# Adding epsilon to the softmax row sums on ScalarE instead of VectorE, and idle matrix products of 64 rows instead of 128

## The chip, the cores and the metric

The kernel runs on one core of one Trainium2 chip. The metric is the device time of one execution in microseconds (us), the median of several runs. A core has five engines that work side by side, each through its own list of instructions in order: TensorE (PE in the profile; PEld are its weight loads), VectorE (DVE), ScalarE (ACT), GpSimd (POOL) and SyncE (SP, which here only issues transfers). They wait for each other through semaphores. TensorE writes to PSUM, which has eight banks of 128 partitions by 512 fp32 words; everything else lies in SBUF.

## The reference

Three stages follow each other, in fp32:

```python
# attention: q, k, v of shape (2, 8, 1152, 64); q is averaged over pairs of tokens first
q_pool = q.reshape(B, H, S // 2, 2, D).mean(axis=3)
scores = matmul(q_pool, k.T) / sqrt(D)
attn = exp(scores - scores.max(-1))
attn = attn / (attn.sum(-1) + 1e-09)
x = matmul(attn, v)                      # then (1152, 512): tokens by heads
# gated MLP, d_ff 1536
x = (silu(x @ w_gate) * (x @ w_val)) @ w_out
# second MLP, d_ff 2048, with a slope alpha below zero
h = x @ w_in
out = (maximum(h, 0) + alpha * minimum(h, 0)) @ w_out2
```

The change is about the `+ 1e-09`, and about products that compute nothing.

## The kernel before, in words

**The order of the work.** The program doesn't issue instructions as it goes through its loops. Each step is handed to a planner (`Plan`, by `add`): engine, guessed duration, priority, what it reads and writes, and a function that emits the instructions. `Plan.run` then plays through time with these guesses and emits every step in the order in which it started in that play. TensorE's steps go strictly by priority. The other engines take the best step that is ready, or hold still for a better one if it will be ready within a short time (0.217 us for ACT, 0.095 us for DVE). A step given to `EITHER` (L730) goes to ACT or DVE, whichever is free. On the chip the order of each engine is then fixed; only the waits decide when a step runs.

**Attention** goes over eight pairs of heads (pair 0 to 7). The planner knows a shared resource between DVE and POOL: a step with `port=True`, and every POOL step, holds it alone. For one pair:

- `prep` loads q, k, v and splits q and k into a high and a low part for products of higher precision. For pair 0 this is done by ACT and DVE, for the others by POOL: L608 writes the high part, L616 the low part (for k these are tiles of 128x1152).
- `unit` computes scores of 128 queries by 1152 keys: matrix products L686 (and L678) into PSUM, then L692 on DVE (scaling, row minimum, copy into SBUF), then L696 on ACT (exp, with the row sum written by ACT into one column of `allsums`).
- `transposed` transposes the exps 64 keys at a time by products with the identity (L716), and ACT (L731) or DVE (L726) copies each filled bank back to SBUF as `et` and `eu`.
- `values` multiplies them with v (L751); ACT copies the result out (L755).
- `inverses` runs once per pair when the last exp of the pair has left its sum: L762 adds epsilon to the 128x9 sums on DVE, L763 takes the reciprocal on DVE into `allinv`, L764 transposes it on TensorE, L765 copies it to SBUF on ACT, and SP sends it through DRAM so that it comes back spread over partitions (L769, L772). `finish` multiplies (L781 on POOL; for the last pair L779 on DVE).

**The idle products.** Until the first `values` step is placed, TensorE gets a product of zeros into bank 7 whenever no step of its own is ready in the play (`plan.idle`, guessed at 0.12 us). It is `idle(256)`: 256 columns, 128 rows, bf16. Ahead of all steps stand 20 products `idle(512)` (`K["warm"]`). Nothing reads what they write.

**The two MLPs** follow from 210.7 us on, with weights that ACT and DVE rebuild from 64-bit words (L527 to L535) beside the products L842, L902 and L931.

Of the kernel before, what the change touches and what calls it, by code (L numbers as in the profile page):

```python
# [9 lines left out]
F32 = mybir.dt.float32  # L10
F32R = mybir.dt.float32r
I32 = mybir.dt.int32
AF = mybir.ActivationFunctionType
ALU = mybir.AluOpType
# [3 lines left out]
P = 128  # L18
PE, ACT, DVE, POOL, SP = "PE", "ACT", "DVE", "POOL", "SP"
# [68 lines left out]
class Plan:  # L88
# [34 lines left out]
    def buf(self, cls):  # L123
        b = Buf()
        c = self.classes[cls]
        b.cls, b.n, b.users, b.slot, b.until = cls, len(c["bufs"]), 0, None, 0.0
        c["bufs"].append(b)
        c["open"] += 1
        return b


    def add(self, eng, dur, emit, prio, reads=(), writes=(), bufs=(), extra=0.0, port=False, late=0.0, hold=0.0, cold=2.0, kind=None):
        t = Task()
        t.kind = kind
        t.eng, t.dur, t.extra, t.emit, t.prio = eng, dur, extra, emit, prio
        t.n, t.ways = len(self.tasks), None
        t.port, t.late = port or eng == POOL, late
        t.after, t.done, t.start, t.hold, t.cold = [], None, None, hold, cold
        deps = set()
        for k in reads:  # L140
            deps.update(self.wr.get(k, ()))
        for k in writes:
            deps.update(self.wr.get(k, ()))
            deps.update(self.rd.get(k, ()))
        for k in writes:
            self.wr[k] = [t]
            self.rd[k] = []
        for k in reads:
            self.rd.setdefault(k, []).append(t)
        deps.discard(t)  # L150
        t.left = len(deps)
        for d in deps:
            d.after.append(t)
        t.ready = 0.0
        t.bufs = list(dict.fromkeys(bufs))
        for b in t.bufs:
            b.users += 1
        self.tasks.append(t)
        return t
# [158 lines left out]
def tp(n):  # L318
    return n * 0.109 / 128.0
# [15 lines left out]
def act(n, sbuf=False, acc=False):  # L335
    return n / 1200.0 + (0.093 if sbuf else 0.051) + (0.186 if acc else 0.0)
# [15 lines left out]
def attention_moe_moe2(  # L352
# [13 lines left out]
    nc = tc.nc  # L366
    NP, _, _, SQ = qt.shape
    S = kt.shape[2]
    D = vt.shape[4]
# [5 lines left out]
    EPS = 1e-9  # L375
# [12 lines left out]
    const = ctx.enter_context(tc.tile_pool(name="const", bufs=1))  # L388
# [5 lines left out]
    signs = const.tile([P, 2, NF2], F32, name="signs")  # L394
    tiny = const.tile([P, 1], F32, name="tiny")
    nc.gpsimd.memset(tiny, 1e-10)
    xh = const.tile([P, KC, NT], F32R, name="xh")
    xl = const.tile([P, KC, NT], F32R, name="xl")
    bank = psum.tile([P, 8, 512], F32, name="bank")
# [4 lines left out]
    zeros = const.tile([P, 512], mybir.dt.bfloat16, name="zeros")  # L404
    nc.vector.memset(zeros, 0.0)

    def idle(n):
        nc.tensor.matmul(bank[:, 7, :n], zeros[:, :P], zeros[:, :n], start=True, stop=True)  # L408

    for i in range(K["warm"]):  # L410
        idle(512)

    plan = Plan()
    plan.first = K["begin_at"]
    plan.cold = K["cold"]
    plan.idle = lambda: idle(256)
    add, buf = plan.add, plan.buf


# [337 lines left out]
    def inverses(x, pos, rd):  # L757

        rows_ = []

        t, r9 = buf("s"), buf("r9")
        add(DVE, 0.097, lambda: nc.vector.tensor_scalar(x.sums.ap, x.sums.ap, EPS, None, ALU.add), pos, rd, [x.sums], [x.sums])  # L762
        add(DVE, 0.097, lambda: nc.vector.reciprocal(x.inv.ap[:, :NU], x.sums.ap), pos, [x.sums], [x.inv], [x.sums, x.inv])  # L763
        add(PE, tp(P), lambda: nc.tensor.transpose(t.ap[:, :P], x.inv.ap, ident), pos, [x.inv], [t], [t, x.inv])  # L764
        add(ACT, act(P), lambda: nc.scalar.activation(r9.ap, t.ap[:NU, :P], AF.Copy), pos, [t], [r9], [t, r9])  # L765
        for j in range(2):
            for dst, src in ((lambda j=j: x.row.ap[j:j + 1, :D], lambda j=j: r9.ap[0:1, j * D:j * D + D]),
                             (lambda j=j: x.row.ap[j, D:].rearrange("(u p) -> u p", p=P), lambda j=j: r9.ap[1 + 4 * j:5 + 4 * j])):
                add(SP, 0.5, lambda dst=dst, src=src: nc.sync.dma_start(dst(), src()), pos, [r9], [(x.row, j, dst)], [x.row, r9], extra=0.02)  # L769
                rows_.append((x.row, j, dst))  # L770
        for j, h in enumerate((slice(0, D), slice(D, P))):
            add(SP, 0.5, lambda j=j, h=h: nc.sync.dma_start(x.rr.ap[h], x.row.ap[j].partition_broadcast(D)), pos, rows_, [(x.rr, j), (x.rr, "q")], [x.rr, x.row], extra=0.41)  # L772
# [16 lines left out]
    for p in range(NP):  # L789
        x = prep(p)  # L790
        x.sums, x.inv, x.row = buf("sums"), buf("inv"), buf("row")
        ets = [[[buf(cls) for cls in ET] for _ in range(2)] for _ in range(2)]
        for g in ets:
            for h in g:
                for b in h:
                    b.parts = []
        xs = buf("xs")
        at = 0
        for g in range(2):
            for n in (OF if p else OF0)[g]:  # L800
                pos = 4.0 * p + 4.0 * (at + 0.5 + 0.5 * (n > 0)) / 9
                at += 1 + (n > 0)
                kinds, es = unit(x, p, n, pos)
                transposed(x, p, n, kinds, es, ets[g], pos)
            if g == 1:
                inverses(x, pos + rank("inv", p, 0), [(x.sums, n) for n in range(NU)])
            values(x, g, ets[g], xs, 4.0 * p + 2.0 * g + 1.0)
        finish(x, p, xs, 4.0 * p + 4.0 + rank("fin", p, 0))
# [201 lines left out]
```

## Time and profile before

| what | value |
|---|---|
| median of 3 runs | 642.7 us (642.59 to 643.03) |
| the profiled execution | 642.54 us |
| its span in the trace | 640.7 us (1.84 us lie outside it) |
| busy share: PE, DVE, ACT, POOL | 99%, 75%, 52%, 16% |
| mean granted TensorE clock | 0.997 of full speed |

The span is the time from the first to the last recorded instruction. Busy time of TensorE is modelled from pipelined products, so 99% says that it has nearly always something in flight, not that it runs at its peak. The profile names a line, an engine, the tiles written and read (`out<-in`), a count, and in brackets the idle time of that engine ahead of it with what ended it.

### The profile page before, as it was taken

Reading aid. Unit: us, or ns where it says so; the run is one execution under the profiler, and the core shown is the slowest. Engines: PE = TensorE matmul, PEld = TensorE weight load, DVE = VectorE, ACT = ScalarE, POOL = GpSimd, SP = SyncE. Lnnn points to the kernel's source line nnn. Section 1 sums busy time; section 2 is a strip of 40 time slices with the busy share of each in tenths; the row PEclk is TensorE's granted clock in tenths of the full one; section 3 lists DMA queues with packets and bytes.
Section 4 is the critical chain, followed back from the end, with each engine's and each line's share of the span. In section 5 each row is a group of like instructions: output and inputs, shape, how many; then the busy total and the mean of one; then the engine's idle time right before and its main releaser. Section 6 shows DMA issues by size and latency. Waiting matters only on the chain.

```text
span 640.7 us, 12340 instructions
## 1 busy us (share of the span) xinstructions
PE 634.6 (99%) x4901; PEld 557.8 (87%) x4901; DVE 478.6 (75%) x1012; ACT 334.9 (52%) x604; POOL 104.4 (16%) x114
## 2 busy tenths in 40 slices
PE   9989999999999999999999999999999999999998
PEld 5777777777776999999999999999988898899886
DVE  6898988988889999988548866688996299463332
ACT  4858887887889535445334222313864454342210
POOL 4543554456204000000000000051000000000000
PEclk9989999999999999999999999999999999999999
DMA  6222322221133434352311420113124011000012
GB/s 223 75 85 85 95 85 85 95 94 39 58 112 107 150 131 132 135 194 72 128 66 68 178 84 19 47 66 132 66 99 165 0 67 67 0 1 2 0 50 98
DMA packets 16874, 55.37 MB, mean 86 GB/s; under 512 B 2160, under 2 KB 3120, under 8 KB 16816
## 3 DMA queue, kind: packets, MB, share of 16 engines
q1 hardware_dynamic: 16672, 54.35, 24.8%
q8 instruction: 38, 0.62, 0.4%
q14 instruction: 20, 0.16, 0.1%
q10 hardware_dynamic: 144, 0.23, 0.1%
HBM read 52.17 MB, written 2.40 MB: 85 GB/s over the span
## 4 chain that ended last, share of the span: by engine, by line
PE 97%; ACT 1%; DVE 1%; issue 1%; DVEq 0%; ACTq 0%
PE bank L842 39%; PE bank L931 16%; PE bank L902 12%; PE bank L751 11%; PE bank L686 9%; PE bank L716 7%; PE bank L678 2%; PE bank L408 2%; ACT plain L696 1%; DVE allsums L762 0%; ACT spare L696 0%; PE bank L764 0%; ACT et L731 0%; DVE plain L692 0%; DVE plain L939 0%
## 5 line engine op out<-in xcount | busy, mean ns | idle before, releaser
L842 PE MATMUL bank<-xh,weights 128*128 128x384 f32 x960 | 253.3, 337 | 0.0
L842 PEld LDWEIGHTS bank<-xh,weights 128*128 128x128 f32 x960 | 174.4, 188 | 2.2 <-issue 0.4
L842 PE MATMUL bank<-xl,weights 128*128 128x384 f32 x480 | 161.4, 336 | 0.0
L842 PEld LDWEIGHTS bank<-xl,weights 128*128 128x128 f32 x480 | 90.2, 188 | 1.2
L696 ACT ACTIVATE plain<-plain,stats 128x1152 f32<-128x1152 f32 x51 | 63.8, 1254 | 15.8 <-DVE plain L692 15.8
L931 PE MATMUL bank<-wr,fed 128*128 128x512 f32 (+1 forms) x279 | 70.4, 387 | 0.0
L686 PE MATMUL bank<-fed 64*128 64x448 f32 (+1 forms) x576 | 65.0, 356 | 0.1
L882 ACT ACTIVATE plain<-bank,signs 128x384 f32<-128x384 f32 x48 | 27.9, 581 | 69.5 <-PE bank L842 69.3
L931 PEld LDWEIGHTS bank<-wr,fed 128*128 128x128 f32 x279 | 51.1, 188 | 10.4
L692 DVE TENSOR_SCALAR_CACHE_REDUCE plain<-bank,stats 128x448 f32<-128x448 f32 (+1 forms) x102 | 55.9, 580 | 2.1 <-PE bank L686 0.9
L883 DVE SCALAR_TENSOR_TENSOR plain<-bank,signs,plain 128x384 f32<-128x384 f32 x48 | 29.5, 614 | 36.2 <-ACT plain L882 36.2
L686 PEld LDWEIGHTS bank<-fed 64*128 64x128 f32 x576 | 48.4, 189 | 6.1 <-issue 1.6
L902 PE MATMUL bank<-fed,wr 128*128 128x384 f32 x264 | 52.2, 338 | 0.0
L716 PEld LDWEIGHTS bank<-ident,plain 64*128 64x128 f32 x918 | 37.9, 139 | 11.4 <-issue 5.5
L911 POOL TENSOR_SCALAR xh<-plain 128x384 fp32r<-128x384 f32 x12 | 13.3, 1110 | 206.8 <-DVE plain L909 206.8
L902 PEld LDWEIGHTS bank<-fed,wr 128*128 128x128 f32 x264 | 46.8, 188 | 0.0
L716 PE MATMUL bank<-ident,plain 64*128 64x64 f32 x918 | 43.5, 228 | 1.7 <-DVE eu L726 1.6
L931 PE MATMUL bank<-wr,h 128*128 128x512 f32 (+1 forms) x165 | 44.3, 389 | 0.0
L527 ACT ACTIVATE magnitudes<-plain 128x1024 f32<-128x1024 f32 x34 | 38.8, 1143 | 9.7 <-DMA plain<-in_w_in 4.5
L751 PE MATMUL bank<-et,plain 128*64 128x320 f32 (+1 forms) x320 | 42.8, 412 | 0.0
L530 DVE SCALAR_TENSOR_TENSOR magnitudes<-plain,magnitudes 128x1024 int32<-128x1024 int32 x34 | 41.4, 1217 | 0.2
L531 DVE SCALAR_TENSOR_TENSOR magnitudes<-plain,magnitudes 128x1024 int32<-128x1024 int32 x34 | 41.4, 1217 | 0.2
(83 smaller groups left out, 936.8 us busy)
## 6 DMA issues: line engine op xcount, KB each, us to landing
plain<-in_w_out SPq DMA_DIRECT2D x28, 512.0 KB
plain<-in_w_in SPq DMA_DIRECT2D x16, 512.0 KB
plain<-in_w_gate SPq DMA_DIRECT2D x12, 512.0 KB
plain<-in_w_val SPq DMA_DIRECT2D x12, 512.0 KB
plain<-in_vt SPq DMA_DIRECT2D x8, 576.0 KB
plain<-in_qt SPq DMA_DIRECT2D x7, 576.0 KB
plain<-in_kt SPq DMA_DIRECT2D x7, 576.0 KB
plain<-rowd SPq DMA_DIRECT2D x16, 144.0 KB
```

The lines of the kernel that those rows point to most:

```text
L527: add(ACT, act(2 * DM, True), lambda: nc.scalar.activation(mag.ap, word(1, F32), AF.Abs), prio, reads=got, writes=[mag], bufs=[raw, mag])
L530: add(DVE, dve(2 * DM), lambda: nc.vector.scalar_tensor_tensor(bits(), word(0, I32), 29, bits(), ALU.logical_shift_right, ALU.bitwise_or), ...
L531: add(DVE, dve(2 * DM), lambda: nc.vector.scalar_tensor_tensor(bits(), word(1, I32), -0x40000000, bits(), ALU.bitwise_and, ALU.bitwise_or) ...
L686: nc.tensor.matmul(ss[h].ap[:, :w], x.qhl.ap[rows, a * SQ + c0:a * SQ + c0 + P], x.khl.ap[rows, b * S + js.start:b * S + js.stop], start=k ...
L692: add(DVE, dve(w) + (0.067 if i else 0.01), lambda s=s, js=js, w=w, i=i, m=m, e=e: nc.vector.tensor_scalar(e.ap[:, js], s.ap[:, :w], QSCAL ...
L696: add(ACT, act(S, True, True), lambda e=e, st=st, u=u: nc.scalar.activation(e.ap, e.ap, AF.Exp, bias=st.ap[:, NCUT - 1:NCUT], scale=-1.0, ...
L716: nc.tensor.transpose(ts[h].ap[:, c * D:c * D + D], e.ap[rows, ks:ks + P], ident[rows, rows])
L751: nc.tensor.matmul(acc.ap[rows, :n], x.vn.ap[:, h * SQ + kc * D:h * SQ + kc * D + D], ets[h][blk].ap[:, at:at + n], start=kc == 0, stop=kc ...
L842: nc.tensor.matmul(acc.ap[:, :TB], l[:, cs], r[:, c, ts], start=c == 0 and a == 0, stop=c == KC - 1 and a == 2)
L883: add(DVE, dve(TB) + 0.056, lambda: nc.vector.scalar_tensor_tensor(u.ap, a.ap[:, :TB], sign(), u.ap, ALU.mult, ALU.max), prio, [a], [u], [ ...
L902: nc.tensor.matmul(acc.ap[:, :TB], l[:, os_], r, start=n == 0 and m == 0, stop=n == len(g) - 1 and m == 2)
L931: nc.tensor.matmul(acc.ap[:, :width], l, r[:, cols], start=n == 0 and m == 0, stop=n == len(g) - 1 and m == 2)
```

## The change

The addition L762 becomes an ACT instruction: the identity function with a per-partition bias, which is a new 128x1 tile `eps` filled once by GpSimd. The planner's guess for the step is 0.22 us in place of 0.097 us. The reciprocal behind it stays on DVE. Second, `idle` gets a number of rows: the 20 products ahead of all steps keep 128, those that the planner puts in get 64 (`D`).

```diff
+    eps = const.tile([P, 1], F32, name="eps")
+    nc.gpsimd.memset(eps, EPS)
...
-    def idle(n):
-        nc.tensor.matmul(bank[:, 7, :n], zeros[:, :P], zeros[:, :n], start=True, stop=True)
+    def idle(n, rows=P):
+        nc.tensor.matmul(bank[:, 7, :n], zeros[:rows, :P], zeros[:rows, :n], start=True, stop=True)
...
-    plan.idle = lambda: idle(256)
+    plan.idle = lambda: idle(256, D)
...
-        add(DVE, 0.097, lambda: nc.vector.tensor_scalar(x.sums.ap, x.sums.ap, EPS, None, ALU.add), pos, rd, [x.sums], [x.sums])
+        add(ACT, 0.22, lambda: nc.scalar.activation(x.sums.ap, x.sums.ap, AF.Identity, bias=eps), pos, rd, [x.sums], [x.sums])
```

## Rows read from the trace of the kernel before

**Rows 1.** The page's clock line: 40 slices of 16 us, tenths of full speed.

```profile
PEclk9989999999999999999999999999999999999999
```

**Rows 2.** The chain that ended last, steady pairs: start us, duration us, what.

```profile
53.84 4.46 PE bank L751 x32
77.81 4.46 PE bank L751 x32
```

**Rows 3.** The same chain around the end of pair 0.

```profile
33.82 1.81 PE bank L716 x32
35.63 2.45 PE bank L686 x12
...
46.08 1.28 PE bank L686 x12
```

**Rows 4.** The timeline there: start, duration, instruction, [idle before <-releaser].

```profile
30.52 2.62 POOL L616 TENSOR_TENSOR fed<-plain,fed 128x1152 fp32r<-128x1152 f32 x1
30.60 2.58 DVE L762 TENSOR_SCALAR allsums<-allsums 128x9 f32<-128x9 f32 x1 [1.93 <-ACT plain L696]
...
30.66 0.46 PE L716 MATMUL bank<-ident,plain 64*128 64x64 f32 x8
30.77 0.44 ACT L755 ACTIVATE plain<-bank 128x320 f32<-128x320 f32 x1 [0.21 <-PE bank L751]
...
31.65 0.52 PE L716 MATMUL bank<-ident,plain 64*128 64x64 f32 x10
...
33.11 1.15 POOL L608 TENSOR_SCALAR fed<-plain 128x1152 fp32r<-128x1152 f32 x1
...
33.27 0.22 DVE L763 RECIPROCAL allinv<-allsums 128x9 f32<-128x9 f32 x1
33.41 0.69 DVE L726 COPY eu<-bank 128x256 f32<-128x256 f32 x2
...
33.82 1.81 PE L716 MATMUL bank<-ident,plain 64*128 64x64 f32 x35 [1.65 <-DVE eu L726]
```

**Rows 5.** All eight executions of L762: duration ns min/median/max.

```profile
L762 DVE TENSOR_SCALAR allsums<-allsums x8: 163/173/2575, 30.6 to 203.6; 128x9 f32<-128x9 f32 x8
```

**Rows 6.** Windows: length, busy of PE, PEld, DVE, ACT, POOL (count), PE clock, DMA share, GB/s.

```profile
34.00:34.50 0.50, 0.50 (x18) 0.49 (x17) 0.50 (x3) 0.14 (x1) 0.42 (x2) 1.00 0.85 111
...
35.00:35.50 0.50, 0.50 (x14) 0.50 (x11) 0.50 (x2) 0.48 (x2) 0.50 (x1) 0.50 0.80 332
...
38.50:39.00 0.50, 0.50 (x6) 0.14 (x2) 0.50 (x3) 0.00 (x0) 0.33 (x3) 1.00 1.02 295
```

**Rows 7.** Windows: two stages from pair 0 into pair 1.

```profile
33.82:38.10 4.28, 4.28 (x50) 3.73 (x52) 3.71 (x12) 1.56 (x4) 4.20 (x3) 0.60 0.50 150
38.10:51.50 13.40, 13.40 (x180) 10.42 (x182) 12.43 (x43) 10.45 (x22) 0.95 (x4) 1.00 0.24 76
```

**Rows 8.** The timeline at the end of pair 1.

```profile
58.72 0.66 ACT L731 ACTIVATE eu<-bank 128x256 f32<-128x256 f32 x2 [0.53 <-PE bank L716]
...
58.75 0.42 DVE L726 COPY eu<-bank 128x256 f32<-128x256 f32 x1 [0.36 <-PE bank L716]
```

**Rows 9.** A small ACT instruction and the first table load: count | busy, mean ns | idle before.

```profile
L765 ACT ACTIVATE rows<-bank 9x128 f32<-9x128 f32 x8 | 2.1, 263 | 1.6 <-PE bank L764 1.6
L403 ACT ACT_TABLE_LOAD x1 | 1.3, 1283 | 0.7 <-PEq L999 0.7
```

**Rows 10.** The timeline of ACT and DVE at the end of pair 7.

```profile
203.38 1.10 ACT L532 ACTIVATE weights<-magnitudes 128x1024 fp32r<-128x1024 f32 x1
...
204.32 0.20 DVE L763 RECIPROCAL allinv<-allsums 128x9 f32<-128x9 f32 x1
```

**Rows 11.** All products of zeros: duration ns min/median/max, first and last start.

```profile
L408 PE MATMUL bank<-zeros x57: 272/283/634, 1.2 to 23.1; 128*128 128x256 bf16 x37, 128*128 128x512 bf16 x20
```

**Rows 12.** The chain's first and longest of 13 runs of idle products.

```profile
8.24 0.22 PE bank L408
...
11.19 0.87 PE bank L408 x7
```

## The prediction

> **What bounds the kernel now.** I read the page first: PE busy 99% of the span and nearly alone in the chain, so a change on DVE or ACT counts only where TensorE stands still, or where it runs at the lower clock. The second view is the chain in order of time. In the steady pairs it holds products alone, and one pair follows the other after 77.81 - 53.84 = 23.97 us [rows 2]: there TensorE sets the time. At the end of pair 0 the chain leaves TensorE for L762, the very line that moves. The third view, the timeline, says why [rows 4]. L762 starts at 30.60 on nine elements per partition and takes 2.58 us, till 33.18. POOL's L616 started at 30.52 and ended at 30.52 + 2.62 = 33.14. The other executions took about 0.17 us (median 173 ns, longest 2575) [rows 5]. So this one addition was held up by about 2.4 us, and let go when the POOL instruction ended. DVE works in order: the reciprocal and the copies L726 stood behind it. TensorE ended its transposes at 31.65 + 0.52 = 32.17, needed a bank that L726 had yet to empty, and stood still for 1.65 us until 33.82 [rows 4].
>
> A second loss follows. The granted clock was 1.00 up to 34.5, 0.50 (1.2 instead of 2.4 GHz) in the window at 35, and 1.00 again at 38.5 [rows 6]. The mean from 33.82 to 38.10 was 0.60 [rows 7]: 0.40 x 4.28 = 1.7 us of full clock were lost there. It lies in the only slice that the page's line of the clock shows below 0.9 [rows 1], and before it TensorE had done transposes and then nothing for 1.65 us.
>
> **The addition, in pair 0.** What it removes: DVE no longer holds the instruction that waits for POOL. Two terms.
>
> First the standstill: **1.65 us** [rows 4].
>
> Second the clock, if it no longer falls. The 12 products L686 took 2.45 us at the low clock and take 1.28 us at the full one: 1.17. The 36 transposes behind the standstill took 1.81 us [rows 3]; the 36 ahead of it ran from 30.66 to 32.17 [rows 4], 1.51: 0.30. Together **1.47 us** (bound from above: the 1.7 of the mean clock).
>
> Does DVE allow it? Its copies could start when the first transposes end, 30.66 + 0.46 = 31.12, plus 0.22 for the reciprocal: about 31.3 instead of 33.41 [rows 4], 2.1 us earlier. That alone gives 2.1. From 33.82 to 51.50 DVE was busy 3.71 + 12.43 = 16.14 of 17.68 us [rows 7]; the idle 1.54 us can shrink, since some of it was waiting for slow products. So DVE bounds the gain of pair 0 between 2.1 and 2.1 + 1.54 = 3.6 us, and the 3.12 of the two terms lie inside.
>
> Does the reciprocal take over the wait? It ran at 33.27 while POOL's L608 ran from 33.11 to 34.26, and took 0.22 us [rows 4]. It is not held by that instruction; that L616, with two inputs, wouldn't hold it either isn't shown.
>
> What it adds: one ACT instruction per pair on 128x9. The trace has no such form; the nearest row is L765 on 9x128 with 263 ns [rows 9]. I take 0.27 us, with bounds of 0.17 (DVE's median) [rows 5] and 0.5 (twice the row, for a wait behind the exp that writes the sum). In pair 0 the Identity comes right behind the last exp or behind L755, which runs at 30.77 after 0.21 us of idle ACT time [rows 4]. So between 0.06 and 0.27 us of it push ACT's copies of the banks that TensorE needs next. I take **0.25 us** against the gain.
>
> **The addition, in pairs 1 to 6.** There ACT is idle for 0.53 us before its first copy, waiting for the transposes, and DVE for 0.36 us before its own [rows 8]. The Identity lies in that gap. If the gap were gone it would cost 0.27 us in each, 1.6 us in all. I take 0. DVE's 0.17 us, gone from there, were hidden as well. The step issues no transfer, and SP's list keeps its order.
>
> **The addition, in pair 7.** ACT starts a weight step L532 of 1.10 us at 203.38 and the reciprocal ran at 204.32 [rows 10]. If the Identity is placed behind L532 it ends at about 204.48 + 0.27 = 204.75, and the reciprocal with all DVE copies behind it is 0.4 us late. Bounds 0 and 0.6; I take **0.2 us**.
>
> **A rule against the change.** The row says 0.27 us on ACT against 0.17 on DVE [rows 5, 9], 0.1 us more in each of eight places, 0.8 us in all if nothing hides them and no addition ever waited; what decides is the one that waited. The Trainium skill's page "ScalarE: Activation LUTs", Rules for kernel authors, says that an add belongs on VectorE, and its section What ACT_TABLE_LOAD costs puts an ACTIVATE with a bias tile at about 280 ns plus 0.83 ns per element, an estimate of 0.29 us here. By that rule alone the kernel would be some 8 x (0.29 - 0.17) = 1.0 us slower; no run here shows it so far.
>
> **The idle products.** 37 of them, from 8.24 on, with 256 columns [rows 11]. A run of one costs 0.22 us in the chain, a run of seven 0.87 [rows 12]: 0.108 us for each and 0.11 for changing over. Columns are unchanged, so the 0.108 stays. If products of 64 rows change over for nothing to those of the kernel, which have 64 rows too [rows 3, 4], 13 runs give back up to 1.4 us of TensorE's time. But they fill time in which TensorE waits for DVE or ACT, so most of it turns into waiting. Value taken 0; bounds a gain of 0.6 and the loss of the slower rival. The new `eps` tile is one POOL instruction of about 0.1 us in the first 2 us, ahead of anything that waits for POOL: 0.
>
> **The sum.** 1.65 + 1.47 - 0.25 - 0.2 = 2.67 us. Made against the profiled execution: 642.54 (span 640.7 + 1.84) - 2.67 = 639.87. The median stands 0.16 above the profiled execution. I say **639.9 us**.
>
> **The rivals.** A change of 0.2%, 1.3 us, is about what a measurement here can tell from none.
>
> *The clock falls all the same* (chance 0.14). Before the fall stood 36 transposes, a standstill and more transposes; if the standstill was not what mattered, the 1.47 are not won: 642.54 - 1.65 + 0.45 = 641.3. For it: 72 transposes will now stand together. Against it: steady pairs with long runs of transposes have no fall.
>
> *The gain is absorbed* (0.10). The planner sees another duration on another engine, so steps given to ACT or DVE may change sides in every later pair, and copies come late for TensorE. With 0.3 us in each of seven pairs, 2.1 of 2.67 are gone: 642.0. Against it: the reciprocal's place in the plan hardly moves, 0.22 on ACT instead of 0.097 and a wait on DVE.
>
> *Slower: the idle products no longer keep the clock up* (0.08). Place: 8 to 24 us. The clock's line shows 0.9 or more in the two slices to 32 us [rows 1], with products of 128 rows between the kernel's own; with 64 rows it could fall. Every us at 0.50 costs 0.5 us of work, and one fall like that at 35 us lasted about 3.4 us, so 1.7 us. Two falls eat the gain; to end 1.3 us above 642.7 takes (2.67 + 1.3) / 0.5 = 8 us at 0.50, half of that stretch: 644 and more. Against it: the clock rose again by 38.5 while TensorE did L716 and L686, all of 64 rows [rows 3, 6].
>
> *ACT reloads its function table* (0.02). One load of 1.28 us stands ahead of all of attention, and exp (L696) and copy (L765) both work with it [rows 9]. If Identity weren't in it, two loads in each of eight pairs, 20 us, partly hidden: 650 and more.
>
> *The opening gains too* (0.06). The change-over times are won: up to 0.6 more, plus the upper bounds of pair 0: 638.6.
>
> *The forecast* (0.60): 638.7 to 640.8.
>
> **How the numbers follow.** Faster by over 0.2% is below 641.4: forecast 0.60, the opening 0.06, the better half of the clock's case 0.08: 0.74. Within 0.2%: the absorbed case and the rest of the clock's, 0.16. Slower: 0.08 and 0.02, 0.10. The range goes from 638.6 (the opening's gain) to 641.8 (the clock's case and part of the absorbed one).
>
> **What the profile would show.** No L762 on DVE, and an ACT instruction on `allsums` of 0.2 to 0.3 us; the reciprocal of pair 0 at about 31.2; copies L726 from there on; PE without a standstill at 32.2; the clock at 1.00 from 30 to 40; the distance of the steady pairs still 23.97; the idle products 37 in number, with 64 rows, clock at 1.00 through 24 us. The prediction is wrong if the reciprocal now lasts 2 us beside L616, if the clock is at 0.50 anywhere in the first 40 us, or if L751 of pair 1 doesn't come some 2.7 us earlier than 53.84.

## The result, and the profile after

The changed kernel took 636.41 us (636.38 to 636.87, 4 runs), the one before 642.72 us (642.59 to 643.03, 4 runs). The ratio is 0.9903, with a 95% interval from 0.9886 to 0.992: faster by 6.3 us, where 2.7 had been forecast. The time lies below the stated range, which began at 638.6. The profiled execution took 636.40 us, with a span of 634.6 where 640.7 stood before.

What was forecast for the end of pair 0 is there. The timeline of the changed kernel (lines moved: L762 to L764, L763 to L765, L726 to L728, L616 to L618):

```profile
28.69 2.65 POOL L618 TENSOR_TENSOR fed<-plain,fed 128x1152 fp32r<-128x1152 f32 x1
28.81 0.30 ACT L764 ACTIVATE allsums<-allsums,eps 128x9 f32<-128x9 f32 x1
...
29.02 0.42 ACT L757 ACTIVATE plain<-bank 128x320 f32<-128x320 f32 x1
...
29.21 0.22 DVE L765 RECIPROCAL allinv<-allsums 128x9 f32<-128x9 f32 x1 [2.39 <-ACT allsums L764]
29.35 0.72 DVE L728 COPY eu<-bank 128x256 f32<-128x256 f32 x2
...
29.79 1.85 PE L718 MATMUL bank<-ident,plain 64*128 64x64 f32 x46
```

Against [rows 4]: POOL's subtraction begins as before and lasts as long, ACT adds epsilon beside it in 0.30 us, the reciprocal runs while POOL is at work and takes 0.22, so it is not held, and the copies follow at once. The transposes have no idle time ahead of them. The page's clock line and two windows of the same stretch say that the clock no longer falls (against [rows 1, 6, 7]; the column before the last two is the granted clock):

```profile
PEclk9999999999999999999999999999999999999999
```

```profile
28.81:32.03 3.22, 3.22 (x79) 3.06 (x79) 2.81 (x9) 3.20 (x10) 3.22 (x2) 1.00 0.12 48
32.03:36.31 4.28, 4.28 (x43) 3.00 (x41) 4.10 (x16) 1.00 (x2) 3.08 (x2) 1.00 0.53 150
```

But this is half of the gain. The chain gives the starts of pair 1 and pair 2 (against [rows 2]):

```profile
48.84 4.46 PE bank L753 x32
72.80 4.46 PE bank L753 x32
```

Pair 1 starts 53.84 - 48.84 = 5.0 us earlier, and the distance of the pairs is 23.96 as before. The table cuts the span of every profiled kernel at the same four places: the start of the first score product and of the first L751 (timeline of TensorE), the start of pair 1's L751 and of the first product of the MLPs (chain). All in us; the ratio is to the kernel before as run beside it.

| kernel | median | ratio (95%) | first score product at | opening, to first L751 | pair 0, to pair 1's L751 | rest of attention | MLPs, to the end |
|---|---|---|---|---|---|---|---|
| before | 642.72 | | 6.96 | 18.70 | 28.18 | 156.82 | 430.04 |
| changed | 636.41 | 0.9903 (0.9886-0.992) | 7.92 | 15.90 | 25.02 | 156.90 | 428.86 |
| epsilon on ACT alone | 638.99 | 0.9936 (0.9923-0.9948) | 6.92 | 18.69 | 25.03 | 156.91 | 428.95 |
| 64 rows alone | 640.06 | 0.9959 (0.9945-0.9973) | 7.34 | 15.91 | 28.15 | 156.84 | 430.06 |
| no idle products | 635.48 | 0.9882 (0.9869-0.9896) | 7.83 | 15.29 | 25.06 | 156.90 | 428.82 |
| 32 rows | 638.92 | 0.9939 (0.9927-0.9952) | 7.38 | 18.93 | 25.02 | 156.91 | 428.86 |
| 64 rows, tile unused | 640.37 | 0.9946 (0.9933-0.996) | 8.00 | 15.93 | 28.35 | 157.01 | 429.51 |
| tile of 64 bytes | 637.17 | 0.99 (0.9886-0.9913) | 7.27 | 15.90 | 25.04 | 156.86 | 429.73 |
| no epsilon, no tile | 637.54 | 0.9908 (0.9894-0.9921) | 7.23 | 15.92 | 25.04 | 156.97 | 430.64 |
| k's low part in 4 | 640.66 | 0.9955 (0.9943-0.9968) | 7.08 | 18.68 | 25.19 | 156.90 | 430.65 |
| accumulator form | 640.50 | 0.9958 (0.9945-0.997) | 8.13 | 18.70 | 25.02 | 157.19 | 430.06 |
| port told | 648.22 | 1.008 (1.0066-1.0093) | 7.14 | 18.69 | 27.02 | 162.07 | 430.68 |
| no idle, no epsilon | 635.51 | 0.9882 (0.9869-0.9896) | 7.55 | 15.29 | 25.01 | 157.01 | 428.94 |
| the same, 16 ahead | 635.16 | 0.9876 (0.9863-0.989) | 6.70 | 15.83 | 25.02 | 157.05 | 428.90 |

From the first to the second line: the start +0.96, the opening -2.80, pair 0 -3.16, the rest +0.08, the MLPs -1.18; the sum is -6.1, the difference of the spans. The start isn't the change's: the 20 products of zeros ahead of all steps are the same in both, and took from 5.8 to 7.0 us in the profiles of the table that have 20 of them, with either part of the change or without. Pair 0 was forecast. The opening and the MLPs were not, and the experiments below are about all three.

### The profile page after: what moved, and what is told of

Its sections match the earlier page's. It is cut to its first block, busy times and chain, and to the rows that moved or that the text cites. A ratio compares the mean times of both kernels' runs of the same rounds, so it can differ in the third digit from the quotient of the medians.

```text
span 634.6 us, 12328 instructions
## 1 busy us (share of the span) xinstructions
PE 630.1 (99%) x4901; PEld 556.0 (88%) x4901; DVE 474.3 (75%) x1004; ACT 336.1 (53%) x612; POOL 103.9 (16%) x115
## 4 chain that ended last, share of the span: by engine, by line
PE 99%; ACT 0%; issue 0%; DVE 0%; ACTq 0%
PE bank L844 40%; PE bank L933 16%; PE bank L904 12%; PE bank L753 12%; PE bank L688 9%; PE bank L718 7%; PE bank L680 2%; PE bank L410 2%; PE bank L766 0%; ACT et L733 0%; ACT spare L698 0%; DVE plain L941 0%; ACT eu L733 0%; ACT plain L757 0%; DVE zeros L407 0%
## 5 line engine op out<-in xcount | busy, mean ns | idle before, releaser
L753 PE MATMUL bank<-et,plain 128*64 128x320 f32 (+1 forms) x320 | 42.8, 411 | 0.1
```

The lines of the kernel that those rows point to most:

```text
L753: nc.tensor.matmul(acc.ap[rows, :n], x.vn.ap[:, h * SQ + kc * D:h * SQ + kc * D + D], ets[h][blk].ap[:, at:at + n], start=kc == 0, stop=kc ...
```

## The experiments

**Each part alone.** Epsilon on ACT, idle products with 128 rows:

```diff
-    plan.idle = lambda: idle(256, D)
+    plan.idle = lambda: idle(256)
```

> Epsilon on ACT, idle products with 128 rows as before. Theory A (the two parts are separate: the addition gains what pair 0 loses in its standstill and at the low clock, the rows gain in the opening): about 642.7 - 3.2 = 639.5 us, pair 0 from its first L751 (25.7) to that of pair 1 about 25.0 us long instead of 28.2, first L751 still near 25.7. Rival B (the addition alone brings the whole gain, and the earlier first L751 is chance of the clock's rise): about 636.4 us.

And 64 rows, with L762 on DVE and no tile `eps`:

```diff
-        add(ACT, 0.22, lambda: nc.scalar.activation(x.sums.ap, x.sums.ap, AF.Identity, bias=eps), ...)
+        add(DVE, 0.097, lambda: nc.vector.tensor_scalar(x.sums.ap, x.sums.ap, EPS, None, ALU.add), ...)
```

> Idle products with 64 rows, epsilon still on DVE. Theory A: the first L751 comes about 1.8 us earlier, the addition is still held till a POOL instruction ends, PE stands still and the clock falls: 642.7 - 1.8 (to - 3) = 639.7 to 640.9 us. Rival B: 642.7 us, no change. Rival C (the idle products set when L762 meets POOL, so the shift alone frees it): 637 us or less and L762 under 0.3 us everywhere.

Measured: 638.99 and 640.06 us, beside 642.96 for the kernel before. The first is 0.5 below what theory A gave, the second inside its range. The table separates the two parts cleanly. With epsilon on ACT pair 0 is 25.03 us long and the opening unchanged at 18.69; with 64 rows the opening is 15.91 and pair 0 unchanged at 28.15. Both rivals B are out. Rival C too: pair 0 began 2.4 us earlier (25.66 against 23.25 for the first L751), and L762 met the same POOL instruction, as the timeline of the kernel with 64 rows alone shows:

```profile
28.11 2.63 POOL L616 TENSOR_TENSOR fed<-plain,fed 128x1152 fp32r<-128x1152 f32 x1
28.18 2.58 DVE L762 TENSOR_SCALAR allsums<-allsums 128x9 f32<-128x9 f32 x1 [1.93 <-ACT plain L696]
...
31.42 1.84 PE L716 MATMUL bank<-ident,plain 64*128 64x64 f32 x34 [1.65 <-DVE eu L726]
```

The MLPs, which neither part seems to touch, are 428.95 us with the first part and 430.06 without it.

**What holds L762.** The kernel before, with POOL's subtraction for the low part of k in four instructions:

```diff
-            add(eng, dur, lambda go=go: go(part(1, c, r), src(c, r), part(0, c, r)..., ALU.subtract), ...)
+            n = 1 if first or what == "q" else 4
+            cs = [slice(c.start + w * m // n, c.start + w * (m + 1) // n) for m in range(n)]
+            def low(go=go):
+                for c in cs:
+                    go(part(1, c, r), src(c, r), part(0, c, r)..., ALU.subtract)
+            add(eng, dur, low, ...)
```

> The kernel before, with POOL's subtraction for the low part of k cut into four instructions of 288 columns, about 0.8 us each. Theory F (L762 is held until the POOL instruction that is running ends): L762 of pair 0 takes 0.3 to 0.9 us instead of 2.58, PE doesn't stand still at the end of pair 0, the clock stays at 1.00, about 639.5 us. Rival G (L762 is slow for another reason, such as its code being fetched, or it waits until POOL has nothing to do): 2.6 us or more, 642.7 us.

640.66 us, with pair 0 at 25.19. The timeline (L762 is L769 here):

```profile
30.61 3.07 POOL L621 TENSOR_TENSOR fed<-plain,fed 128x288 fp32r<-128x288 f32 x4
30.68 0.74 DVE L769 TENSOR_SCALAR allsums<-allsums 128x9 f32<-128x9 f32 x1 [1.92 <-ACT plain L703]
```

The addition ends at 31.42, when the first of the four can have ended (30.61 + 3.07 / 4 = 31.38), not at 33.68 with the last. So what holds it is the one POOL instruction that is running, and rival G is out. The median stands 1.1 us above the 639.5 of theory F: pair 0 has its gain, but the first 336 products of the MLPs took 0.6 us longer in this profile (see below), and the kernel before took 643.42 us beside it, 0.7 more than in the result.

**The form of the addition.** The kernel before, with epsilon on DVE at the same place, by an instruction that also writes an accumulator which nobody reads:

```diff
-  nc.vector.tensor_scalar(x.sums.ap, x.sums.ap, EPS, None, ALU.add)
+  nc.vector.tensor_scalar(x.sums.ap, x.sums.ap, EPS, None, ALU.add, ALU.min, accum_out=spill)
```

> The kernel before, with epsilon still added on DVE at the same place, but by the form of L692, which also writes an accumulator (a minimum that nobody reads). Theory F1 (it is the form of the instruction that makes it wait for POOL): L762 about 0.2 us everywhere, no standstill, 639.5 us. Rival (any DVE instruction from SBUF to SBUF waits while POOL subtracts): 2.6 us in pair 0, 642.7 us.

640.50 us, beside 643.14 for the kernel before, and pair 0 at 25.02. It is 1.0 above the 639.5 of theory F1; in its profile the first score product came at 8.13 us instead of 6.96. The timeline (L762 is L763, L616 is L617):

```profile
31.70 2.64 POOL L617 TENSOR_TENSOR fed<-plain,fed 128x1152 fp32r<-128x1152 f32 x1
31.76 0.17 DVE L763 TENSOR_SCALAR_CACHE_REDUCE allsums<-allsums 128x9 f32<-128x9 f32 x1 [1.93 <-ACT plain L697]
```

Same engine, same operands, same meeting with POOL, and 0.17 us instead of 2.58. It is the form that is held, not DVE. The reciprocal, never held, is a third witness. The Trainium skill's page "SBUF — State Buffer", section Who interferes with whom, says the same: a plain `tensor_scalar` can enter a mode that takes the port pair shared with GpSimd, the form that writes out its accumulator can't, and whoever starts first keeps the pair for the whole instruction. All three statements agree with these traces (2.58, 0.17 and 0.74 us).

**Another order instead of another engine.** The kernel before, with the planner told that L762 needs the shared resource:

```diff
-        add(DVE, 0.097, ..., pos, rd, [x.sums], [x.sums])
+        add(DVE, 0.097, ..., pos, rd, [x.sums], [x.sums], port=True)
```

> The kernel before, with the planner told that L762 needs what DVE and POOL share, so it lets DVE do its copies first and adds epsilon when POOL is idle in its play. If the standstill is the loss: L762 under 0.3 us, no fall of the clock, 639.5 to 640.5 us (the reciprocal of pair 0 comes several us later, so L764 may hold TensorE). If the addition finds POOL at work all the same: 2.6 us once, but with the copies ahead of it, 640 to 642 us.

648.22 us, slower by 0.8%, outside all that was expected. L762 is never held (157 to 177 ns), but the planner puts that of pair 0 behind all DVE copies of the pair and 13 steps L692 of the next, and the transpose of the reciprocals, which has its fixed place in TensorE's order, waits. A line of the waits (total, times, longest) and the timeline:

```profile
PE bank L764 <- DVE allinv L763: 5.3, 2, 3.6
```

```profile
41.47 0.22 DVE L763 RECIPROCAL allinv<-allsums 128x9 f32<-128x9 f32 x1
...
41.74 0.33 PE L764 MATMUL bank<-ident,allinv 128*128 128x128 f32 x1 [1.71 <-DVE allinv L763]
```

Pair 0 loses 2 us of its gain (27.02), and the rest of attention 5.2 (162.07), of which 3.6 are the other of the two waits, at the end of pair 7. Behind that wait the granted clock fell to 0.50; behind the wait of 1.71 us in pair 0 it did not. A fall that cost 1.7 us, as the prediction reckoned for the one of the kernel before (an estimate), would make up the rest of the 5.2. A line of the timeline and two windows:

```profile
208.03 0.30 PE L764 MATMUL bank<-ident,allinv 128*128 128x128 f32 x1 [3.56 <-DVE allinv L763]
```

```profile
38.00:42.00 4.00, 2.29 (x15) 1.55 (x11) 3.90 (x17) 3.46 (x7) 2.11 (x4) 1.00 0.48 147
210.00:212.00 2.00, 2.00 (x12) 1.18 (x10) 2.00 (x3) 1.19 (x4) 0.00 (x0) 0.50 0.52 163
```

So a standstill of TensorE as long as the 1.65 us of [rows 4] doesn't make the clock fall by itself. Ahead of the two falls stood transposes and a wait (1.65 and 3.56 us), ahead of the wait without a fall stood score products. No run tells what decides.

**The rows of the idle products.** The changed kernel without the 37 products, and with 32 rows:

```diff
-    plan.idle = lambda: idle(256, D)
+    plan.idle = lambda: None            # the one kernel
+    plan.idle = lambda: idle(256, 32)   # the other
```

> Epsilon on ACT, and none of the 37 idle products that the planner puts in; the 20 ahead of all steps stay. If the products of 64 rows still cost TensorE time on the way to the first L753, it comes earlier than 23.9 us by up to 0.5 and the time is 636.0 or less. If they cost nothing but also keep no clock up: 636.4. If they hold the clock, it falls to 0.50 somewhere before 30 us and the time is 638 us or more.

> As the changed kernel, but idle products of 32 rows. Theory A1 (what counts is that the rows are those of the neighbours, so that TensorE needn't change over from one shape to another): the cost of 0.11 us per run is back, first L753 1 to 1.8 us later, 637.5 to 638.5 us. Theory A2 (fewer rows are cheaper, or leave rows free for the neighbour): 636.4 us or a little less. In both, a clock of 0.50 before 30 us would say that 32 rows don't hold it.

Without them 635.48 us, as expected of products that still cost time, with the first L753 0.70 us earlier (0.5 at most had been expected). With 32 rows 638.92, slower than theory A1 expected: its 0.11 us per run was too little. The opening is 18.70 with 128 rows, 18.93 with 32, 15.90 with 64, and 15.29 with none. So theory A1 holds in this: what counts is that the shape is that of the neighbours, not that there are fewer rows. The timelines of TensorE show where the cost sits: idle runs and what follows them, before, then after, then with 32 rows.

```profile
8.17 0.28 PE L408 MATMUL bank<-zeros 128*128 128x256 bf16 x1
8.38 0.71 PE L686 MATMUL bank<-fed 64*128 64x448 f32 x6
...
11.12 0.94 PE L408 MATMUL bank<-zeros 128*128 128x256 bf16 x7
11.99 0.87 PE L686 MATMUL bank<-fed 64*128 64x448 f32 x6
...
14.88 0.39 PE L408 MATMUL bank<-zeros 128*128 128x256 bf16 x2
15.03 0.86 PE L678 MATMUL bank<-fed,corner 128*128 128x448 f32 x3
```

```profile
9.03 0.28 PE L410 MATMUL bank<-zeros 64*128 64x256 bf16 x1
9.04 0.82 PE L688 MATMUL bank<-fed 64*128 64x448 f32 x7
...
11.13 0.72 PE L410 MATMUL bank<-zeros 64*128 64x256 bf16 x5
11.58 0.47 PE L688 MATMUL bank<-fed 64*128 64x448 f32 x1
11.68 0.38 PE L410 MATMUL bank<-zeros 64*128 64x256 bf16 x2
11.82 0.84 PE L688 MATMUL bank<-fed 64*128 64x448 f32 x5
...
14.06 0.38 PE L410 MATMUL bank<-zeros 64*128 64x256 bf16 x2
14.37 0.88 PE L680 MATMUL bank<-fed,corner 128*128 128x448 f32 x3
```

```profile
8.60 0.28 PE L410 MATMUL bank<-zeros 32*128 32x256 bf16 x1
8.80 0.71 PE L688 MATMUL bank<-fed 64*128 64x448 f32 x6
...
11.53 0.93 PE L410 MATMUL bank<-zeros 32*128 32x256 bf16 x7
12.39 0.87 PE L688 MATMUL bank<-fed 64*128 64x448 f32 x6
```

These are distances between starts, and within a run idle products start 0.11 to 0.12 us apart. From a single idle product to the score product behind it lie 0.21 us with 128 rows, 0.20 with 32, and 0.01 with 64. For L678 with its 128 rows it is the other way round: it starts 0.15 us behind the first of two idle products of 128 rows, and 0.31 behind the first of two of 64. Less the distance of the two that is 0.03 us behind products of the same shape and 0.20 behind those of another.

The 0.01 is something else besides: it is less than the 0.11 us that an idle product takes, so the score product did not wait for it. The run of seven says it more plainly. The play doesn't know the rows, so the order of issue is the same in all three kernels, seven idle products and then the scores. With 64 rows the first score product starts ahead of the last two of the seven, and the other five behind them. By the kernel's text the scores of `unit` come in pairs, one on rows 0 to 63 and one on rows 64 to 127, and `zeros[:64]` lies on the first; so the early one is most likely that of the other half, running beside the idle products. With 32 rows the second half is free as well, and yet nothing starts early. How much of the gain comes from the missing change of shape, and how much from working side by side, no run separates.

The clock did not need the idle products in the opening: windows of the kernel without them, TensorE busy for 6.84 and 7.48 of 8 us.

```profile
8.00:16.00 8.00, 6.84 (x65) 5.10 (x66) 7.25 (x28) 4.50 (x9) 2.79 (x3) 1.00 0.57 195
16.00:24.00 8.00, 7.48 (x116) 6.14 (x116) 7.95 (x28) 6.95 (x18) 3.74 (x7) 1.00 0.23 77
```

**Where the MLPs got faster.** The kernels with a tile of one word in the place of `eps` have MLPs near 428.9 us, those without it 430.0; some entries of the table stand 0.6 above either, for a reason given below. The groups by shape, of the kernel before and then of the changed one (busy, mean ns):

```profile
L931 PE MATMUL bank<-wr,fed 128*128 128x512 f32 x261 | 67.9, 395 | 0.0
L902 PE MATMUL bank<-fed,wr 128*128 128x384 f32 x264 | 52.2, 338 | 0.0
```

```profile
L933 PE MATMUL bank<-wr,fed 128*128 128x512 f32 x261 | 67.3, 393 | 0.0
L904 PE MATMUL bank<-fed,wr 128*128 128x384 f32 x264 | 51.6, 335 | 0.0
```

The products are the same, 2 to 3 ns shorter each. The tile `eps`, one word wide, lies ahead of `fed` in SBUF and moves it, by 32 bytes as the expectations have it (the traces hold no addresses). Two kernels test that: 64 rows, epsilon on DVE, and `eps` filled but unused; and the changed kernel with `eps` 16 words wide.

```diff
+    eps = const.tile([P, 1], F32, name="eps")             # the one, with L762 on DVE
-    eps = const.tile([P, 1], F32, name="eps")
+    eps = const.tile([P, 16], F32, name="eps")[:, 0:1]    # the other
```

> The kernel before with idle products of 64 rows and the new tile eps filled but used by nothing; epsilon is still added on DVE. The tile moves every later tile of SBUF by 32 bytes. Theory D (the 1.1 us that the MLP stage is shorter in all kernels with eps come from that move): about 640.1 - 1.1 = 638.9 us, L902 from the tile fed at 335 ns instead of 338, and L762 still held for 2.58 us. Rival E (they come from another order of ACT and DVE steps): 640.1 us, 338 ns.

> The changed kernel, with eps widened so that the later tiles move by 64 bytes instead of 32. Theory D, with what counts being the place within 64 bytes: L904 from fed at 338 ns again, 636.4 + 1.1 = 637.5 us. If any move will do: 335 ns, 636.4. Rival E (order of steps): 335 ns, 636.4.

The medians, 640.37 and 637.17 us, are 3.05 and 6.25 below the 643.42 of the kernel before beside them. Taken alone, the first is nearer to rival E (640.1) than to theory D (638.9), but starts that differ by 1 us can't settle a matter of 1.1 us. The stages can. Three stretches of the MLPs, read in the chain, have the same length to 0.02 us in every profile of one placement: the 156 products L902 at the end of the first MLP, the mixed stretch of L931 and L842 in the second, and the last 120 products L931.

| placement | 156 L902 | mixed | 120 L931 | profiles |
|---|---|---|---|---|
| no tile | 27.39 | 144.36 | 25.26 | 6 |
| 32 bytes | 27.13 | 143.65 | 25.09 | 7 |
| 64 bytes | 27.26 | 144.13 | 25.04 | 1 |

The kernel with the unused tile is among the seven, with L762 held for 2.58 us as ever. Theory D holds, rival E falls: 0.26 + 0.71 + 0.17 = 1.14 us come from the place of the tiles. The kernel with 64 bytes says the same: its instructions are those of the changed kernel, and only the width of the tile differs. With 64 bytes part of it is lost, so not any move will do, but that the place within 64 bytes decides is not borne out either: its three stretches lie between the two others or below them. Which operand it is, and why, stays open. Apart from that, the first 336 products of the MLPs took 58.5 us in some profiles and 59.1 in others, across placements; that is why some entries of the table stand 0.6 higher.

**What the Identity on ACT costs.** The changed kernel without the addition, and without the tile (the sums are at least 1, so that in fp32 the epsilon left out changes nothing):

```diff
-        add(ACT, 0.22, lambda: nc.scalar.activation(x.sums.ap, x.sums.ap, AF.Identity, bias=eps), ...)
```

> The changed kernel without the addition of epsilon, on any engine, and without its tile (the sums are at least 1, since each row's largest exp is 1). Tells what the Identity on ACT costs. Theory A with D (ACT's eight instructions are hidden but for some 0.2 us, and the missing tile puts the MLP stage back): 637.2 to 637.6 us, attention up to the first L842 as long as in the changed kernel. If the Identity is on the path at several places: 636.5 or less.

637.54 us, as forecast with the tile's 1.1 us gone. That the median fits so well is partly luck: in its profile the start is 0.7 us earlier than in the changed kernel's, and the first 336 products of the MLPs take 0.6 longer. The stages decide. Pair 0 is 25.04 us and the rest of attention 156.97, where the changed kernel has 25.02 and 156.90. So the eight instructions are hidden, to 0.1 us.

**Versions that beat both.** The changed kernel without idle products and without the addition, a tile of 32 bytes kept; and the same with `warm=16` instead of 20:

> A version to beat both: no idle products from the planner, no addition of epsilon on any engine (the sums are at least 1), a tile of 32 bytes kept so that the later tiles stay where they are in the changed kernel. Without idle products the changed kernel took 635.5 us; if the Identity costs nothing this is 635.5 as well, if it costs its 0.3 us in pair 0, 635.2.

> As the kernel without idle products and without the addition, with 16 products of zeros ahead of all steps instead of 20. They ended at 7.0 to 8.0 us in the runs so far, while the data for the first score products were there at 7.0: up to 0.9 us earlier, 634.6 to 635.3 us. If the clock then rises later or falls in the opening: 635.5 us or more.

635.51 and 635.16 us. The first equals the kernel without idle products that still adds epsilon (635.48), which again prices the Identity at nothing. In the second the first score product starts at 6.70 instead of 7.55, but the opening is 15.83 instead of 15.29: of the 0.85 us most is waited for later, and 0.3 are left at the first L751 (22.53 against 22.84). Its median is the lowest, though the intervals of the two overlap.

## Why the prediction was wrong

- *L762 is held by POOL's instruction, and its loss is the standstill and the fall of the clock.* Right, and now shown by three kernels that free it in different ways: pair 0 takes 25.02 us on ACT, 25.02 with the other form, 25.19 with shorter POOL instructions. The two terms less the delay on ACT made 1.65 + 1.47 - 0.25 = 2.87; measured 28.18 - 25.02 = 3.16. The delay of 0.25 was not there. In the three profiles in which L762 was held for 2.58 us (before, 64 rows alone, tile unused) the clock fell behind it, in the others it did not fall there; so the two terms came and went together, and no run tells them apart.
- *The Identity.* Taken at 0.27 us, measured 0.30 (303 to 316 ns). The Trainium skill's estimate of 0.29, from "ScalarE: Activation LUTs", What ACT_TABLE_LOAD costs, was nearer. That page's rule that an add belongs on VectorE did not bear on the time, since all eight are hidden; the 0.2 for pair 7 were too much too, the rest of attention lost 0.08 in all.
- *The step that failed: the idle products, "Value taken 0; bounds a gain of 0.6".* The sentence before had the price of changing over and its removal right, up to 1.4 us for 13 runs, and then let it turn into waiting for DVE and ACT. The opening shrank by 2.80 us. Two things were wrong there. It was taken for granted that filled time is spare time. But the chain that [rows 12] come from holds TensorE's products alone from 8.24 to 24.40 us, 5.3 us of idle runs among them, and without any filling the opening is 15.29 us long. So the products of 128 rows cost 18.70 - 15.29 = 3.4 us, those of 64 rows 0.6, and only the rest of the 5.3 was spare. And the price was too small: 0.11 us is what an idle run adds in the chain ahead of its end, while the product behind the run starts late as well (0.20 us behind the last idle product instead of 0.03). On average 3.4 / 13 = 0.26 us go with each run, an estimate that puts all of the loss down to the runs' ends. That a score product may also start beside idle products of its own shape was not in the prediction at all. The Trainium skill's page "TensorEngine Tiling (Array Packing)", Key Properties, says that changing the tiling mode drains TensorE. The 0.20 us against 0.03 above agree, and this rule should have raised the chance of the rival in which the opening gains too.
- *What the sum lacked: the tile.* It was costed as one POOL instruction, at nothing. Its room moved the operands of the MLPs, and gave 1.14 us; why the place matters stays open.
- *The rivals.* The clock did not fall with 64 rows, nor with none; ACT reloaded no table; the later pairs kept their 24 us. "The opening gains too" had the right mechanism in part, sized at 0.6 us instead of 2.8.

## What to carry to other kernels

Work that only fills an engine's time still has a price where it meets real work: give filling products the shape of their neighbours, and time the kernel without them before tuning them. A short instruction with a long maximum in a group's durations may be waiting for something that the waits don't name; look for the instruction of another engine that ends when it does, and try another form of the same operation before another engine or another place in the order. And a new tile, however small, moves all tiles behind it: compare stages that the change doesn't touch before counting their difference as its effect.

## What the runs showed of the hardware

- A product behind an idle product of another shape started 0.20 to 0.21 us after it (128 to 64 rows, 32 to 64, 64 to 128), one of the same 128 rows 0.03 us after it.
- With 64 rows on both sides a score product started 0.01 us after an idle product that takes 0.11, and ahead of two idle products issued before it; with 32 or 128 rows none did.
- A one-source DVE instruction from SBUF to SBUF on nine elements waited 2.4 us for a POOL instruction that subtracts, and 0.74 us in all where that instruction was a quarter as long; the same with an accumulator written out (0.17 us), and the reciprocal (0.22), did not wait.
- fp32 products of 384 and 512 columns ran 2 to 3 ns faster when a tile of one word stood ahead of their operands, 1.14 us over the MLPs, and repeated that to 0.02 us in every profile.
- The granted clock stayed at 1.00 in the opening with TensorE busy for 6.84 of 8 us. It stayed there behind a wait of 1.71 us that followed score products, and fell to 0.50 behind waits of 1.65 and 3.56 us that followed transposes.
